# Two more pairs of heads in the later structure, in an attention and FFN kernel on one core

## The chip, the core and the metric

The kernel runs on one core of a Trainium2 chip. Five engines work side by side, each through its own instructions in order: TensorE (PE) multiplies matrices, VectorE (DVE) and ScalarE (ACT) work elementwise, GpSimd (POOL) does elementwise work more slowly, and SyncE (SP) issues the DMA transfers. The metric is the time of one execution on the device in microseconds (us). A difference under about 0.2% can't be told from no change here.

## What is computed

Attention with a block-causal mask over 8 batches of 8 heads, each 576 rows of 64, in float32; then a two-layer FFN over the 4608 rows of 512 that it yields.

```python
scores = scale * np.matmul(q, k.transpose(0, 1, 3, 2))
scores = np.where(block_i >= block_j, scores, -1000000000.0)      # blocks of 64
scores = scores - np.max(scores, axis=-1, keepdims=True)
attn = np.exp(scores)
attn = attn / (np.sum(attn, axis=-1, keepdims=True) + 1e-09)
x = np.matmul(attn, v)            # then heads side by side: (4608, 512)
h = x @ w_in                      # 512 -> 2048
out = np.maximum(0.01 * h, h) @ w_out
```

## The kernel before

**Heads.** The 64 heads are taken one after the other (`attention(i)`), rows in five tiles of up to 128 (`NT`). A head has scores in two groups (tiles 3 and 2, then 4, 1 and 0), each followed by a maximum over the row (DVE, L537), the exponential with its sum (ACT, L546), the reciprocal (DVE, L562 and L563) and, except in batch 0, the division of the rows (`normalising`, on POOL, DVE or ACT, L576 to L578). The rows are then turned, so that the keys lie on partitions, and a pair of heads is multiplied with v into `xr`, the FFN's input.

**Two structures.** Heads up to `PLAIN` (16 before: batches 0 and 1) use the early one: plain float32 scores from `k_in` and `qk_in` (L505), the rows turned by PE through `ident` (L603) and copied from PSUM to `ptf`, and the product with v in `paired` (L682). It has two sets of row buffers, `prow`. The heads from `PLAIN` on (`flip`) use the later one: q and k come in one load (L483), are split into a high and a low part (`qs`, `ks`), and the scores are products of those parts (L516); the rows are turned in 32 by 32 blocks on DVE into `turn` (L717), go out to `way` in DRAM (L732) and back into `ptm` (L739) so that the blocks land on their partitions, four DMAs each way a head; the product with v is in `columns` (L639). There is one set of `prow` for all of these heads.

**Weights.** `w_in` and `w_out` come as 64-bit words, in 32 pieces. `weight_piece` loads each into one of three `raw` buffers (L419) and decodes it in several steps through `val` (L272, L424, L428, L433 and, for every fifth, L437 and L438) into a high part (`wih`, `woh`) and the rest (`wil`, `wol`).

**FFN.** 18 chunks of 256 rows, each in eight steps u: `ffn1` multiplies x, split into `xh` and `xl`, with two columns of blocks of `w_in` (L795, 24 matmuls), then comes the activation (L810), the split of its result (`gh`, `gl`), and `ffn2` multiplies with `w_out` (L822, twice six matmuls) and adds up in `p_o` over the eight steps. A chunk can start when all heads of the batches that it reaches into are done: chunks 0 and 1 after batch 0, chunks 2 and 3 after batch 1, chunks 4 and 5 after batch 2. Chunks whose batch is done before head `PLAIN` use `xh0` alone; the later ones use `xh0` and `xh1` in turn.

**Memory that changes hands.** The early pool on the left holds the second `prow`, `ptf`, `vf`, `k_in` and `ident`; the coded pool on the right holds `raw` and `val`. At head `PLAIN`, `second_stage` closes the coded pool and puts the pool "late" there, once all weights are decoded; `third_stage` closes the early pool and puts the pool "last" there, once the early heads no longer use it.

**Order.** All steps are handed to `Plan`, which simulates the engines with written-out costs, and issues the instructions in the order that it finds. An operation has a rank; of those ready on an engine the lowest rank goes first. A head i has rank i and offsets of it (`RP`, `RB`, `RT`, `RV`, `RX`, `RN` for the division, `RM` for the DMAs to and from `way`); a weight piece has a rank between `OFF1` and `OFF1 + SL1`; an FFN step that of its head plus `LEAD`. `PADD`, `FILLTO` and `SPARE` are margins and limits within the plan. PE and the other engines each run what they were given in that order, so an instruction that waits holds up those behind it.

Of the kernel before, what the change touches and what calls it, by code (L numbers as in the profile page):

```python
# [9 lines left out]
F32 = mybir.dt.float32  # L10
F32R = mybir.dt.float32r
# [6 lines left out]
P = 128  # L18
BLK = 64
D = 64  # L20
S = 576
# [3 lines left out]
CH = 256  # L25
# [2 lines left out]
SIGNS = 5  # L28

WIDE = 512  # L30
PLAIN = 16
SPREAD = True

RAWS = 3
# [5 lines left out]
RT = 2.029  # L40
RV = 2.563
RX = -1.606
RN = -68.228
RM = -26.73

LEAD = 5.131
LAG = 1.993
RS = -9.988
RG = -0.7
OFF1 = 3.83  # L50
SL1 = 23.573
AHEAD = 2.641

MOVES = {
    "raw": (2200, 675), "first": (3300, 675), "v0": (1600, 900), "k": (900, 1170), "q": (500, 1110), "qk": (1500, 1325), "v": (450, 792),
    "way": (590, 385), "back": (1090, 1095), "out": (690, 354),
}
PADD = 2980.813
HOLD = 261.018
FILL = 235  # L60
FILLTO = -154.639


LOAD = 109
PAD = 510.012
PADO = 9.942
SPARE = 45.103
CHANGE = 100
RATE = 0.449
EDGE = 110  # L70
# [4 lines left out]
class Plan:  # L75
# [19 lines left out]
    def add(self, choices, rank, reads=(), writes=(), lag=None, kind=None):  # L95
        i = len(self.ops)
        deps = set()
        for k in reads:
            if k in self.writer:
                deps.add(self.writer[k])  # L100
        for k in writes:
            if k in self.writer:
                deps.add(self.writer[k])
            deps.update(self.readers.get(k, ()))
        for k in reads:
            self.readers.setdefault(k, []).append(i)
        for k in writes:
            self.writer[k] = i
            self.readers[k] = []
        deps.discard(i)  # L110
        self.ops.append((choices, rank, deps, lag, kind))

    def run(self):
# [16 lines left out]
        def offer(i):  # L130
            for k, choice in enumerate(self.ops[i][0]):
                e = choice[0]
                e = e[:3] if e == "DVE+" else e
                at = max([0] + [ends[d][1] + self.SYNC.get((ends[d][0], e), 0) for d in self.ops[i][2]])
                slack = {e: 0, "SP": PADD}
                spare = PAD if e == "PE" else PADO
# [32 lines left out]
        while done < total:  # L169
# [6 lines left out]
            for e, q in ready.items():  # L176
# [30 lines left out]
                if e == "DVE":  # L207
                    near, far = choices[k][3] if len(choices[k]) > 3 else (0, 0)
                    cost += EDGE * (near != edge)
                    edge = far  # L210
                free[e] = now + cost + SPARE
                if name in ("DVE+", "POOL"):
# [39 lines left out]
def attention_ffn(ctx: ExitStack, tc: tile.TileContext, q2: bass.AP, k2: bass.AP, qk: bass.AP, v: bass.AP, w_in: bass.AP, w_out: bass.AP, out: bass.AP):  # L252
# [3 lines left out]
    ND = DM // P  # L256
# [37 lines left out]
    def fixed(shape, dt, name, n=None, pool=const):  # L294
        if n is None:
            return pool.tile(shape, dt, name=name)
        return [pool.tile(shape, dt, name=f"{name}{i}") for i in range(n)]

    later = {}
# [11 lines left out]
    turned = 4 * BLK // 2 * slots  # L311
# [42 lines left out]
    xh = [fixed([P, ND, CH], F32R, "xh0")]  # L354
# [4 lines left out]
    pool = early.enter_context(tc.tile_pool(name="early", bufs=1, reuse_waits="tile"))  # L359
# [9 lines left out]
    pool = coded.enter_context(tc.tile_pool(name="coded", bufs=1, side="right", reuse_waits="tile"))  # L369
# [3 lines left out]
    def second_stage():  # L373
        coded.close()
        pool = ctx.enter_context(tc.tile_pool(name="late", bufs=1, side="right", reuse_waits="tile"))
        later["qs"] = fixed([P, S], F32R, "qs", 2, pool)
        later["ks"] = fixed([P, 2, S], F32R, "ks", None, pool)

    def third_stage():
        early.close()  # L380
        pool = ctx.enter_context(tc.tile_pool(name="last", bufs=1, reuse_waits="tile"))
        later["ptm"] = fixed([P, turned], F32, "ptm", 2, pool)
        later["turn"] = fixed([P, turned], F32, "turn", 2, pool)
        later["vt"] = fixed([P, NT, D], F32, "vt", 2, pool)
        xh.append(fixed([P, ND, CH], F32R, "xh1", None, pool))

    def weight_piece(num, rank, f, out_side, c0):
        w, k, kv = WIDE, num % RAWS, num % VALS
# [62 lines left out]
    def attention(i):  # L451
        b, h = divmod(i, H)
        z = i % 2
        r0 = float(i)
        flip = i >= PLAIN
        y = 0 if flip else z
# [9 lines left out]
        def pkeys(t):  # L466
            return [("p", y if t else 0, t)]
# [14 lines left out]
        else:  # L482
            add([("SP", ISSUE, lambda: nc.sync.dma_start(qk_in, qk[i - PLAIN]))], r0 - RL, [], ["qkt"], lag="qk")  # L483
            vt, vkey = lambda: later["vt"][z], ("vt", z)
# [37 lines left out]
        def softmax(tiles, mms, masks, r, both=None):  # L522
# [43 lines left out]
            for t, _, _ in () if scaled else tiles:  # L566
                add(normalising(t, qn[t]), r - RN, [("rec", z, at_col[t])], pkeys(t))

        def normalising(t, rr):
            by = rec[z][:rr, at_col[t] : at_col[t] + 1]  # L570

            def p():
                return row(t, rr, pc[t], kw[t])

            return [
                ("POOL", pool1(kw[t]), lambda: nc.gpsimd.tensor_scalar(p(), p(), by, 1.0, op0=ALU.mult, op1=ALU.mult)),  # L576
                ("DVE+", dve(kw[t], True) + 69, lambda: nc.vector.tensor_scalar_mul(p(), p(), by)),
                ("ACT", act(kw[t], True) + 108, lambda: nc.scalar.mul(p(), p(), by)),  # L578
            ]
# [125 lines left out]
    def turn(i, row, pkeys):  # L705
# [24 lines left out]
        for b in range(4):  # L730
            add(
                [("SP", ISSUE, lambda b=b: nc.sync.dma_start(way[z][b], later["turn"][z][:, b * w : (b + 1) * w]))],  # L732
                r0 + RM, ready, [("way", z, b)], lag="way",
            )
        for b in range(4):
# [4 lines left out]

            add([("SP", ISSUE, back)], r0 + RM, [("way", z, b)], [("ptm", z, b)], lag="back")

# [19 lines left out]
    def side(c):  # L762
        return 0 if ready[c] < PLAIN else (c + 1) % 2

    def split_x(c, rank):
        at = c * CH
        z = side(c)
        while at < (c + 1) * CH:
            b, o = divmod(at, S)
            ln = min(S - o, (c + 1) * CH - at)  # L770
            d = at - c * CH
            hi = [("xh", z, e) for e in range(d, d + ln, BLK)]
            keys = [("x", b % 2, h, y) for h in range(H) for y in (0, 1) if (o < 320 if y == 0 else o + ln > 320)]

            def part(which, b=b, o=o, ln=ln, d=d):
                return xr[b % 2][:, :, o : o + ln] if which is None else (xl if which else xh[z])[:, :, d : d + ln]

            x, top, low = (lambda part=part, y=y: part(y) for y in (None, 0, 1))
            add(copying(4 * ln, top, x, first="DVE"), rank, keys, hi)
            add(subtracting(4 * ln, low, x, top)[:1], rank, keys + hi, [("xl", e) for _, _, e in hi])  # L780
            at += ln
# [62 lines left out]
    for num, (f, o, c) in enumerate(pieces):  # L844
        kind = "wo" if o else "wi"
        wkeys.setdefault((kind, f), []).extend([((kind, f, c), 0), ((kind, f, c), 1)])
        weight_piece(num, OFF1 + SL1 * (num + 1) / len(pieces), f, o, c)
    ready = []
    for c in range(NCHUNK):
        b, o = divmod((c + 1) * CH - 1, S)  # L850
# [3 lines left out]
    for i in range(NH + 1):  # L854
        if i == H:
            add([("POOL", 1, narrow)], 0, [], [("h", y) for y in range(2)])
        if i == PLAIN:
            new = [("qs", y) for y in range(2)] + ["kh", "kl"]
            add([("POOL", 1, second_stage)], 0, [y for k in wkeys.values() for y in k], new)
            blocks = ((0, 0), (1, 0), (2, 0), (3, 0), (3, 3), (4, 0), (4, 3), (4, 4))  # L860
            new = [("turn", y, t, j) for y in range(2) for t, j in blocks]
            new += [("ptm", y, b) for y in range(2) for b in range(4)] + [("vt", y) for y in range(2)] + ["qkt"]
            new += [("xh", 1, e) for e in range(0, CH, BLK)]
            old = [("ptf", y, g[0]) for g in tgroups for y in range(2)] + ["ident"]
            old += [(k, y) for k in ("vf", "q", "k") for y in range(2)] + [("p", 1, t) for t in range(1, NT)]
            add([("POOL", 1, third_stage)], 0, [], sorted(set(old), key=str) + new)
        if i in events:
            here = [c for c in range(NCHUNK) if ready[c] == i]
            nxt = events[events.index(i) + 1] if i != events[-1] else i + H
            num = len(here) * NU  # L870
            for k in range(num):
                c, u = here[k // NU], k % NU
                rank = i + LEAD + (nxt - i) * k / num
                if u == 0:
                    split_x(c, rank - RS)
                ffn1(c, u, rank)
                ffn2(c, u, rank + (nxt - i) * LAG / num + 0.003)
        if i < NH:
            attention(i)
    if FILL:  # L880
# [3 lines left out]

        plan.fill = (FILL, fill, 2500, FILLTO)
    plan.run()
# [30 lines left out]
```

## Time and profile before

| | us |
|---|---|
| median of 3 runs (1067.55 to 1068.31) | 1067.56 |
| the profiled execution | 1069.45 |
| its span in the profile | 1067.7 |
| PE busy | 1051.8 |
| DVE busy | 552.7 |
| ACT busy | 549.8 |
| POOL busy | 316.3 |

The span runs from the first to the last instruction of the profiled execution; what lies around it is 1.75 us. The granted clock of PE is 1.00 of full speed, the upper of its two levels (2.4 GHz), in every slice of the page. Busy time is counted while an instruction is in flight; matmuls overlap, so an instruction's length in the trace is longer than what it adds to PE's time, and the distance between two starts is the better measure.

### The profile page before, as it was taken

What the parts mean: (1) busy time and instruction counts of PE and PEld (TensorE: products, weight loads), DVE (VectorE), ACT (ScalarE), POOL (GpSimd) and SP (SyncE); (2) the same over time, 40 slices, a digit from 0 to 9 for tenths busy, and PEclk for the clock granted to TensorE, in tenths of its full rate; (3) what the DMA queues carried; (4) which work ended last, traced back from release to release, by engine and by line L of the source; (5) the groups of instructions that cost most, each with busy time, mean ns of one, the idle gap of its engine ahead of it and who ended that gap; (6) DMA issues with size and microseconds to landing.
All of it is one profiled execution on the core that took longest, in us unless ns stands there. A gap on an engine that the chain in (4) does not pass through costs nothing.

```text
span 1067.7 us, 19239 instructions
## 1 busy us (share of the span) xinstructions
PE 1051.8 (99%) x7072; PEld 914.3 (86%) x7072; DVE 552.7 (52%) x1528; ACT 549.8 (51%) x1327; POOL 316.3 (30%) x304
## 2 busy tenths in 40 slices
PE   7899999999999999999999999999999999999998
PEld 5678888988888888888898888888898888999997
DVE  7998963566566676675444556556655520000000
ACT  7888864654555464554444555555555532222222
POOL 3454332432321222232121233323233322222221
PEclk9999999999999999999999999999999999999999
DMA  6555402776776687786266375667676650000000
GB/s 203 193 167 172 151 34 67 201 218 175 213 214 179 193 226 200 200 237 188 97 179 159 120 204 177 202 177 200 189 214 173 184 147 20 2 21 20 1 20 20
DMA packets 89885, 159.07 MB, mean 149 GB/s; under 512 B 9408, under 2 KB 74944, under 8 KB 89792
## 3 DMA queue, kind: packets, MB, share of 16 engines
q1 hardware_dynamic: 89792, 157.85, 50.7%
q8 instruction: 56, 0.92, 0.4%
q14 instruction: 37, 0.30, 0.1%
HBM read 104.33 MB, written 53.48 MB: 148 GB/s over the span
## 4 chain that ended last, share of the span: by engine, by line
PE 93%; DMA 2%; ACT 2%; DVE 2%; issue 0%; POOL 0%; SPq 0%; ACTq 0%; POOLq 0%
PE p_h L795 37%; PE p_o L822 36%; PE p_s L516 7%; PE p_t L639 6%; PE p_s L505 3%; PE p_t L603 1%; PE p_t L682 1%; DMA qk_in<-in_qk 1%; ACT prow L546 1%; DMA k_in<-in_k 1%; PE p_w L505 1%; DVE nmrec L537 1%; DMA way<-turn 0%; PE p_o L603 0%; DVE val L424 0%
## 5 line engine op out<-in xcount | busy, mean ns | idle before, releaser
L795 PE MATMUL p_h<-xh,wih 128*128 128x256 f32 x1152 | 317.4, 281 | 0.4 <-ACT xh L268 0.4
L795 PE MATMUL p_h<-xh,wil 128*128 128x256 f32 x1152 | 314.3, 278 | 0.0
L283 POOL TENSOR_TENSOR gl<-g,gh 128x512 fp32r<-128x512 f32 x130 | 169.4, 1303 | 468.0 <-ACT gh L268 370.4
L795 PE MATMUL p_h<-xl,wih 128*128 128x256 f32 x1152 | 300.0, 278 | 0.0
L795 PEld LDWEIGHTS p_h<-xh,wih 128*128 128x128 f32 x1152 | 216.5, 188 | 12.5 <-issue 3.2
L795 PEld LDWEIGHTS p_h<-xh,wil 128*128 128x128 f32 x1152 | 217.0, 188 | 0.5
L795 PEld LDWEIGHTS p_h<-xl,wih 128*128 128x128 f32 x1152 | 208.0, 188 | 8.2 <-issue 0.3
L810 ACT ACTIVATE g<-p_h 128x512 f32<-128x512 f32 x144 | 85.9, 597 | 242.3 <-PE p_h L795 242.0
L546 ACT ACTIVATE prow<-p_s,nmrec 128x448 f32<-128x448 f32 x300 | 154.2, 523 | 69.1 <-DVE nmrec L537 68.0
L822 PE MATMUL p_o<-woh,gh 128*128 128x512 f32 x576 | 181.4, 396 | 0.0
L822 PE MATMUL p_o<-wol,gh 128*128 128x512 f32 x576 | 179.3, 392 | 0.0
L822 PE MATMUL p_o<-woh,gl 128*128 128x512 f32 x576 | 179.2, 392 | 0.0
L717 DVE STREAM_TRANSPOSE turn<-prow 128x128 f32<-128x128 f32 (+3 forms) x384 | 143.0, 402 | 49.5 <-POOL prow L576 42.4
L822 PEld LDWEIGHTS p_o<-woh,gl 128*128 128x128 f32 x576 | 108.2, 188 | 24.3
L822 PEld LDWEIGHTS p_o<-wol,gh 128*128 128x128 f32 x576 | 108.2, 188 | 23.5
L537 DVE TENSOR_REDUCE nmrec<-p_s 128x1 f32<-128x448 f32 x300 | 127.5, 469 | 1.2
L576 POOL TENSOR_SCALAR prow<-prow,nmrec 128x448 f32<-128x448 f32 (+3 forms) x98 | 70.4, 720 | 186.1 <-DVE nmrec L563 127.9
L822 PEld LDWEIGHTS p_o<-woh,gh 128*128 128x128 f32 x576 | 89.7, 188 | 4.9 <-issue 2.7
L516 PE MATMUL p_s<-ks,qs 128*128 128x288 f32 (+4 forms) x528 | 91.6, 306 | 0.9 <-ACT prow L546 0.9
L282 DVE TENSOR_TENSOR xl<-xr,xh 128x1024 fp32r<-128x1024 f32 (+3 forms) x24 | 22.6, 950 | 128.2 <-PE p_h L795 128.1
L516 PEld LDWEIGHTS p_s<-ks,qs 128*128 128x128 f32 x528 | 78.9, 188 | 8.8 <-issue 1.9
L268 ACT CAST gh<-g 128x512 fp32r<-128x512 f32 x123 | 76.2, 619 | 19.9 <-PE p_o L822 18.0
(96 smaller groups left out, 995.9 us busy)
## 6 DMA issues: line engine op xcount, KB each, us to landing
way<-turn SPq DMA_DIRECT2D x192, 224.0 KB, 2.5
ptm<-way SPq DMA_DIRECT2D x192, 224.0 KB, 4.6
qk_in<-in_qk SPq DMA_DIRECT2D x48, 576.0 KB, 4.5
out<-ob SPq DMA_DIRECT2D x35, 256.0 KB, 2.6
raw<-in_w_in SPq DMA_DIRECT2D x16, 512.0 KB, 4.3
raw<-in_w_out SPq DMA_DIRECT2D x16, 512.0 KB, 3.8
vt<-in_v SPq DMA_DIRECT2D x48, 160.0 KB, 4.8
vf<-in_v SPq DMA_DIRECT2D x16, 160.0 KB, 2.7
```

Source lines behind the costliest of these rows:

```text
L268: one = lambda: nc.scalar.copy(dst(), src())
L283: ("POOL", pool2(n), lambda: nc.gpsimd.tensor_sub(dst(), one(), two())),
L505: go = lambda ap=ap, cols=cols, k0=k0, k1=k1, first=first, last=last: nc.tensor.matmul(ap, q_of()[:, cols], kt()[:, k0:k1], start=first, s ...
L516: nc.tensor.matmul(ap, later["qs"][z][:, cols], moving, start=first, stop=last)
L537: [("DVE", dve(kw[t]), lambda t=t, ap=ap, flat=flat: nc.vector.tensor_reduce(nm[z][: qn[t], at_col[t] : at_col[t] + 1], ap[: qn[t]], axis= ...
L546: nc.scalar.activation(o, ap[: qn[t]], AF.Exp, bias=nm[z][: qn[t], at_col[t] : at_col[t] + 1], scale=1.0, accum_out=sums[z][: qn[t], at_co ...
L576: ("POOL", pool1(kw[t]), lambda: nc.gpsimd.tensor_scalar(p(), p(), by, 1.0, op0=ALU.mult, op1=ALU.mult)),
L639: nc.tensor.matmul(dst, later["vt"][z][:, j], src, start=start, stop=stop)
L717: nc.vector.transpose(dst, src.rearrange("p (s b i) -> p s b i", b=4, i=32))
L795: nc.tensor.matmul(p_h[z][:, i, :], w[:, d, f * P : (f + 1) * P], (xl if x else xh[y])[:, d, :], start=first and k == 0 and (u > 0 or i == ...
L810: add([("ACT", act(512), lambda: nc.scalar.activation(g, p_h[z], AF.Prelu, alpha=0.01))], rank, [("h", z)], ["g"])
L822: nc.tensor.matmul(p_o[m], a[:, i, m * P : (m + 1) * P], w[:, 2 * u + i, :], start=u == 0 and k == 0, stop=u == NU - 1 and k == 5,)
```

## The change

`PLAIN` goes from 16 to 12. Heads 12 to 15, the second half of batch 1, take the later structure. `qs` and `ks` move from the pool "late" into the pool "last", and `turn` and `xh1` move from "last" into "late". So `turn` and `xh1` now lie where the weights were decoded, `qs` and `ks` where the early heads had their buffers, and the lists of what each stage hands over change with them. The constants of the plan are set anew, which changes the order of the instructions on every engine.

```diff
-PLAIN = 16
+PLAIN = 12
...
-RN = -68.228
-RM = -26.73
+RN = -79.904
+RM = -25.225
...
-SL1 = 23.573
+SL1 = 24.252
...
-PADD = 2980.813
+PADD = 2346.17
...
-FILLTO = -154.639
+FILLTO = -146.062
...
-SPARE = 45.103
+SPARE = 46.259
...
     def second_stage():
         coded.close()
         pool = ctx.enter_context(tc.tile_pool(name="late", bufs=1, side="right", reuse_waits="tile"))
-        later["qs"] = fixed([P, S], F32R, "qs", 2, pool)
-        later["ks"] = fixed([P, 2, S], F32R, "ks", None, pool)
+        later["turn"] = fixed([P, turned], F32, "turn", 2, pool)
+        xh.append(fixed([P, ND, CH], F32R, "xh1", None, pool))

     def third_stage():
         early.close()
         pool = ctx.enter_context(tc.tile_pool(name="last", bufs=1, reuse_waits="tile"))
         later["ptm"] = fixed([P, turned], F32, "ptm", 2, pool)
-        later["turn"] = fixed([P, turned], F32, "turn", 2, pool)
+        later["qs"] = fixed([P, S], F32R, "qs", 2, pool)
+        later["ks"] = fixed([P, 2, S], F32R, "ks", None, pool)
         later["vt"] = fixed([P, NT, D], F32, "vt", 2, pool)
-        xh.append(fixed([P, ND, CH], F32R, "xh1", None, pool))
...
         if i == PLAIN:
-            new = [("qs", y) for y in range(2)] + ["kh", "kl"]
+            blocks = ((0, 0), (1, 0), (2, 0), (3, 0), (3, 3), (4, 0), (4, 3), (4, 4))
+            new = [("turn", y, t, j) for y in range(2) for t, j in blocks] + [("xh", 1, e) for e in range(0, CH, BLK)]
             add([("POOL", 1, second_stage)], 0, [y for k in wkeys.values() for y in k], new)
...
+            new = [("qs", y) for y in range(2)] + ["kh", "kl", "qkt"] + [("vt", y) for y in range(2)]
+            new += [("ptm", y, b) for y in range(2) for b in range(4)]
```

## Rows read from the trace of the kernel before

**Rows 1.** The page: busy time by engine, a costly group, and a DMA's landing.

```profile
PE 1051.8 (99%) x7072; PEld 914.3 (86%) x7072; DVE 552.7 (52%) x1528; ACT 549.8 (51%) x1327; POOL 316.3 (30%) x304
...
L717 DVE STREAM_TRANSPOSE turn<-prow 128x128 f32<-128x128 f32 (+3 forms) x384 | 143.0, 402 | 49.5 <-POOL prow L576 42.4
...
ptm<-way SPq DMA_DIRECT2D x192, 224.0 KB, 4.6
```

**Rows 2.** Waits of PE, the longest: us in total, times, longest us.

```profile
PE p_s L505 <- ACT k_in L271: 4.4, 1, 4.4
```

**Rows 3.** Windows: stretch and length, then busy us of PE, PEld, DVE, ACT, POOL, clock, DMA.

```profile
100.00:150.00 50.00, 50.00 (x317) 40.89 (x316) 43.55 (x99) 37.94 (x94) 17.12 (x14) 1.00 0.39 121
150.00:200.00 50.00, 50.00 (x335) 44.28 (x334) 20.23 (x59) 25.60 (x64) 16.91 (x16) 1.00 0.27 85
```

**Rows 4.** Timeline of PE: start and length in us, line, operation, tiles.

```profile
101.72 1.62 PE L505 MATMUL p_s<-k_in,qk_in 128*128 128x288 f32 x8
103.15 0.71 PE L822 MATMUL p_o<-woh,gh 128*128 128x512 f32 x2
103.71 0.62 PE L822 MATMUL p_o<-wol,gh 128*128 128x512 f32 x2
...
108.77 1.45 PE L505 MATMUL p_s<-k_in,qk_in 128*128 128x448 f32 x4
109.81 0.87 PE L822 MATMUL p_o<-woh,gh 128*128 128x512 f32 x2
110.53 0.63 PE L822 MATMUL p_o<-wol,gh 128*128 128x512 f32 x2
...
111.45 1.04 PE L603 MATMUL p_t<-ident,prow 128*128 128x128 f32 x8
112.24 0.37 PE L795 MATMUL p_h<-xh,wih 128*128 128x256 f32 x1
...
126.71 0.93 PE L603 MATMUL p_t<-ident,prow 128*128 128x128 f32 x7
127.39 0.71 PE L822 MATMUL p_o<-woh,gh 128*128 128x512 f32 x2
...
177.50 0.87 PE L516 MATMUL p_s<-ks,qs 128*128 128x448 f32 x4
...
182.42 1.03 PE L516 MATMUL p_s<-ks,qs 128*128 128x288 f32 x7
183.28 0.62 PE L822 MATMUL p_o<-woh,gh 128*128 128x512 f32 x2
...
188.82 0.86 PE L516 MATMUL p_s<-ks,qs 128*128 128x448 f32 x4
189.52 0.62 PE L822 MATMUL p_o<-woh,gh 128*128 128x512 f32 x2
```

**Rows 5.** The chain that ended last, in order of time: start and length in us.

```profile
118.88 2.84 PE p_t L682 x20
...
164.80 1.40 PE p_o L822 x6
166.20 2.84 PE p_t L682 x20
...
203.69 1.84 PE p_h L795 x16
...
217.71 2.96 PE p_t L639 x28
```

**Rows 6.** Windows of 103 to 143: DVE, ACT, POOL on `val` alone; then all engines.

```profile
103.00:143.00 40.00, 24.65 (x38) 9.07 (x14) 7.78 (x6) 1.00 0.43 132
...
103.00:143.00 40.00, 40.00 (x248) 33.30 (x246) 36.61 (x81) 30.86 (x73) 13.98 (x11) 1.00 0.43 132
```

**Rows 7.** Timelines of POOL (the last weight) and of SP (the first pair's `ptm`).

```profile
141.39 1.65 POOL L283 TENSOR_TENSOR wol<-val,woh 128x512 fp32r<-128x512 f32 x1 [3.67 <-DVE woh L269]
...
206.00 2.40 SPq L739 DMA_DIRECT2D ptm<-way  x4
```

More of the change, by code (lines that the diff above doesn't have):

```diff
@@ L857, in attention_ffn @@
         if i == PLAIN:
-            new = [("qs", y) for y in range(2)] + ["kh", "kl"]
+            blocks = ((0, 0), (1, 0), (2, 0), (3, 0), (3, 3), (4, 0), (4, 3), (4, 4))
+            new = [("turn", y, t, j) for y in range(2) for t, j in blocks] + [("xh", 1, e) for e in range(0, CH, BLK)]
             add([("POOL", 1, second_stage)], 0, [y for k in wkeys.values() for y in k], new)
[L860 to L863, printed above, removed]
+            new = [("qs", y) for y in range(2)] + ["kh", "kl", "qkt"] + [("vt", y) for y in range(2)]
+            new += [("ptm", y, b) for y in range(2) for b in range(4)]
             old = [("ptf", y, g[0]) for g in tgroups for y in range(2)] + ["ident"]
```

## The prediction

> **What bounds the kernel now.** I read the page's first part, then TensorE's (PE's) waits, then the windows, then PE's own timeline. PE is busy 1051.8 of 1067.7 us [rows 1], so 15.9 us of the span is not PE work; the longest wait, 4.4 us, is the first one, on k at the start [rows 2]. From 100 to 200 us PE has no idle time at all, while VectorE (DVE) falls from 43.6 busy us in 100 to 150 to 20.2 in 150 to 200 [rows 3]. So work taken off PE shortens the span, unless PE then waits for something. The whole question is whether it does, and the place to look is 100 to 200 us, where the early structure ends and the later one begins.
>
> A check that PE's time is understood. Sixteen matmuls of the first FFN product take 1.84 us, so a piece of 12 takes 1.38, and a piece of six of the second takes 1.40 [rows 5]; an eighth of a chunk has two of each, 5.56 us, a chunk 44.5, all 18 some 801. That leaves some 250 us for the 64 heads, and only they are touched.
>
> **PE work removed: 11.4 us.** The price of an instruction group is the distance from its start to the start of what follows, since matmuls overlap; a change of structure also slows the group behind it, and that is counted too.
> - An early head has two groups of scores. The eight-matmul one runs 101.72 to 103.15, 1.43 us, and the pair behind it takes 0.56 instead of 0.47 (a third of 1.40), so 1.52. The four-matmul one runs 108.77 to 109.81, 1.04, and the pair behind takes 0.72, so 1.29. [rows 4, 5]
> - It has 15 transposes on PE: 0.79 us for eight and 0.68 for seven [rows 4]. The change behind them I take at the same 0.09 each (the two measured values are 0.09 and 0.25): 1.65. Sum for an early head: 4.46.
> - A later head has 0.70 for four and 0.86 for seven score matmuls, 1.56, and no PE transposes [rows 4].
> - So 2.90 us a head, 11.6 for four. The product with v goes the other way: a pair takes 2.96 instead of 2.84 us [rows 5], 0.24 more for two pairs. Net **11.4 us**. With change-overs of 0.25 behind the transposes it would be 12.7, with none at all 9.7; I keep 11.4.
>
> **Work added elsewhere.** Each of the four heads gets eight DVE transposes at 402 ns, 3.2 us [rows 1], eight more DMA issues on SP (four for `way`, four for `ptm`; four of the latter take 2.40 us [rows 7]), a joint load of q and k, and the split of q and k; it loses the copies of PE's transposes out of PSUM. From 150 us on DVE works 20.2 us of 50 [rows 3], so four times 3.2 us fits there and I cost it at nothing. If it had to run before the weights are decoded, DVE would have no room (43.6 of 50) and it would cost its full length in decoding time; that is the term below. On SP the new loads stand in one queue with the loads of raw weights: a load of q and k that waits for its buffer holds the raw loads queued behind it, and with them the decode.
>
> The transposes take 1.65 us a head on the engine that is 99% busy and 3.2 us on one that is 52% busy [rows 1], so the rows speak for the move. A rule speaks against it: the Trainium skill, VectorE: DVE Perf Modes, section Rules for kernel authors, gives a 128x128 transpose to TensorE where PSUM will do as the target, since VectorE turns 32x32 blocks only. By that rule the four heads would keep their 6.6 us on PE, and the gain would be 4.8 us instead of 11.4.
>
> **What takes the place: the decode of the weights.** `second_stage` puts the transposed rows' buffers (`turn`) where raw and decoded weights lie, so no new head can be turned before the last weight is decoded; today that is at 143.0 (141.39 + 1.65) [rows 7]. Chunk 0 of the FFN needs all the weights as well, and chunk 1 can't begin its second product before chunk 0 is through (one pair of accumulators, and one `xh` for both). So taking heads 12 to 15 out of 103 to 143 us only helps if the decode gets faster.
> - In 103 to 143 DVE works 36.61 us, a share of 0.915; 24.65 of it on weights [rows 6], 11.96 on the rest, most of it heads 12 to 14. The new head 12 can start only near 130 (below). I take a third of the 11.96 to stay: 28.6 us at the same share is 31.3 us, decode ends at **T = 134.3**. None left gives 129.9, all left 143.0: the bounds.
> - From T on PE has: the last eighth of chunk 0's, less its first half, 4.2 us; chunk 1, 44.5; scores of heads 13 to 15, 4.7; two products with v, 5.9; the scores of heads 16, 17 and half of 18, which today also stand ahead of chunk 2, 3.8; less 2.8 of chunk 1 that runs behind the start of chunk 2. Sum 60.3, so chunk 2 starts at 134.3 + 60.3 = 194.6.
> - Today chunk 2 starts at 203.7 [rows 5]; with 11.4 us of work gone and no new idle time it would be 192.3. So **2.3 us of new idle time**. With T at 132.0 or less there is none; with T at 143 it would be 11.0.
>
> **Is the attention there in time?** Chunk 2 is the first to need heads 12 to 15. Today the last early product with v starts at 166.2 and the first scores of the new structure at 177.50, 11.3 us later; the product of that first new pair comes at 217.7, 40.2 later; a head follows the one before by 11.3 us (177.50 to 188.82) [rows 4, 5]. The last early product moves to heads 10 and 11, at 118.9 [rows 5]. So first new scores at 130.2, first pair 170.4, second pair 22.6 later: 193.0. That is what it takes with PE coming late: the last `ptm` transfer of the first new pair is issued by 208.4 [rows 7] and with the median 4.6 us to land [rows 1] it is in at 213.0, 4.7 before PE takes it. So 188.3 to 193.0, and with 3 us for the product chunk 2 can start from 191.3 to 196.0. The decode's 194.6 lies within that, so the two clocks agree, and I keep 2.3. The copy and cast of x hide behind the last 2.8 us of chunk 1.
>
> **Sum.** The profiled execution took 1069.45 us (span 1067.7 and 1.75 around it); less 11.4, plus 2.3: 1060.35. The three runs have a median of 1067.56, 1.89 below the profiled one, so on their scale the forecast is 1067.56 - 9.1 = **1058.5 us**.
>
> **Rivals.**
> - Full gain: the decode ends by 132.0 and the attention keeps its 188.3. For it: DVE and ACT are relieved of three heads just there. Then 1067.56 - 11.4 = 1056.2, and 1055 with the dearer change-overs or a shorter start (15.9 us of idle time, which a new order can shift by a little either way).
> - The attention is late: the steps between heads stretch from 11.3 to 13 us because the new heads start beside the decode. Four steps cost 6.8 us more, so chunk 2 starts between 198.1 and 202.8 instead of 191.3 and 196.0; the middle, 200.5, is 8.2 us of idle time: 1064.3.
> - Slower than before, from one mechanism: the turn of head 12 waits for the decode, and there is one set of `prow` buffers for all new heads, so head 13 can't write its rows until head 12 is turned. Today the product of the first pair comes 35.3 us after the second scores of its first head (182.42), which is about when its turning can start. If the decode still ends at 143.0, the products come at 178.3 and, 22.6 later, 200.9, and chunk 2 at 203.9: the whole gain is gone, 1067.8. From there each us of T costs a us: if head 12's own softmax, which the planner ranks ahead of weights, pushes the decode to 147, the time is 1071.5. For it: DVE is nearly full there today. Against: the new head cannot start until near 130, so it pushes less than the three heads that it replaces.
> - A later hand-over from one batch to the next turns tight because PE comes to it earlier. No row here prices that; it widens the upper end.
>
> **How the numbers follow.** Forecast with 1 to 4.5 us of new idle time, 1057.5 to 1061: 0.54. Full gain, 1055 to 1057.5: 0.16. Attention late, 1061 to 1065.4: 0.13. Gain gone, 1065.4 to 1069.7 (within 0.2%, about what can be told from no change here): 0.09. Slower: 0.08. The range that leaves out no more than 2 in 10 is 1055.5 to 1066. Faster 0.83, same 0.09, slower 0.08.
>
> **What would show it.** Right: PE busy near 1040 us (11 to 12 less), 60 fewer transposes of L603 and 32 more of L717; last write of `wol` between 130 and 138; chunk 2's first group of 16 near 195; some 2 to 4 us of new PE waits between 120 and 200, on weights (`wih`, `woh`) or on `ptm` or `xh`. Wrong: PE's busy time not down by 11 (prices wrong), the last decode at 143 or later, or a wait of PE of over 8 us ahead of chunk 2.

## The result and the profile after

The changed kernel takes **1074.08 us** (median of five runs, 1073.07 to 1076.25) against 1067.77 of the kernel before, measured beside it: 1.0056 times as long, interval 1.0042 to 1.007. It is slower, by 6.3 us. The forecast of 1058.5 was 15.6 us too low, and the range of 1055.5 to 1066 doesn't hold the time. The profiled execution took 1076.25 us, the longest of the five, with a span of 1074.2 (before 1067.7).

The page of the kernel after, the lines that answer to [rows 1]:

```profile
span 1074.2 us, 19255 instructions
...
PE 1052.8 (98%) x7024; PEld 914.0 (85%) x7024; DVE 562.1 (52%) x1558; ACT 550.2 (51%) x1327; POOL 317.1 (30%) x308
...
L717 DVE STREAM_TRANSPOSE turn<-prow 128x128 f32<-128x128 f32 (+3 forms) x416 | 155.7, 403 | 64.5 <-POOL prow L576 53.6
```

PE has 48 instructions fewer and DVE 32 more transposes, as foreseen, and yet PE is busy 1.0 us longer than before instead of 11 less. Its idle time (span less busy) rose too, from 15.9 to 21.4 us.

Windows of after, the stretches of [rows 3] and [rows 6]:

```profile
100.00:150.00 50.00, 49.79 (x329) 43.45 (x328) 44.52 (x88) 33.93 (x75) 16.34 (x13) 1.00 0.45 146
103.00:143.00 40.00, 39.79 (x261) 34.28 (x260) 35.92 (x65) 26.95 (x58) 12.16 (x9) 1.00 0.44 144
150.00:200.00 50.00, 49.15 (x326) 42.83 (x326) 32.01 (x99) 27.97 (x71) 17.59 (x16) 1.00 0.74 206
```

This is where the prediction looked, and hardly anything is lost there: PE idles 1.06 us in 100 to 200. DVE takes the new work in 150 to 200 (32.0 us instead of 20.2) without holding PE up. The loss is elsewhere.

**Where the time went, by line.** Below is a reading of our own of the two traces: for each line of PE the distances from one matmul's start to the next, less the idle time between them, added up (rounded); "ends" is what lies before the first and behind the last matmul. The columns are the kernel before, and the differences from it for after and for two experiments that come below.

```
us                          before   after    e7      e9
L505 early scores             47.8    -9.0   -10.6    -9.8
L603 transposes on PE         26.1    -4.8    -6.0    -5.5
L516 later scores             76.5    +6.9    +6.7    +6.8
L639, L682 products with v    93.6    +0.2    +0.2    +0.2
L795 first FFN product       402.4    +6.4    +1.8    +0.2
L822 second FFN product      400.8    +1.3    -0.5    -0.7
idle between matmuls           7.7    +5.4    +3.5    +6.5
ends, L671                    12.8     0       0      -0.1
span                        1067.7    +6.5    -4.9    -2.6
```

The heads gave back 6.7 us (the first four lines), but the FFN, in which no instruction was changed, takes 7.7 us more, and 5.4 us of idle time are new. A stretch at a lower clock, shown below, adds some 3.4 us to after alone, in L505, L603 and L795; so a part of the 7.7 and of what the heads lack is the clock's. So there are two questions: why the FFN is slower, and where PE idles.

**The FFN's step.** Timeline of PE, single sixteenths of a chunk (12 matmuls of L795, six of L822); start and length in us. First before, in chunk 16:

```profile
978.20 0.28 PE L795 MATMUL p_h<-xh,wih 128*128 128x256 f32 x1
...
979.59 0.62 PE L822 MATMUL p_o<-woh,gh 128*128 128x512 f32 x2
...
980.96 0.28 PE L795 MATMUL p_h<-xh,wih 128*128 128x256 f32 x1
```

After, first in chunk 13, which reads `xh0`, then in chunk 14, which reads `xh1`:

```profile
851.05 0.28 PE L795 MATMUL p_h<-xh,wih 128*128 128x256 f32 x1
...
852.44 0.62 PE L822 MATMUL p_o<-woh,gh 128*128 128x512 f32 x2
...
853.81 0.28 PE L795 MATMUL p_h<-xh,wih 128*128 128x256 f32 x1
...
903.42 0.28 PE L795 MATMUL p_h<-xh,wih 128*128 128x256 f32 x1
...
904.84 0.62 PE L822 MATMUL p_o<-woh,gh 128*128 128x512 f32 x2
...
906.23 0.28 PE L795 MATMUL p_h<-xh,wih 128*128 128x256 f32 x1
```

Twelve matmuls of L795 take 1.39 us before and in chunk 13 of after, but 1.42 in chunk 14; the whole sixteenth 2.76, 2.76 and 2.81. Sixteen times 0.05 is 0.8 us a chunk, and eight chunks (2, 4, ... 16) read `xh1`. The mean step from one L795 matmul to the next is 114.6 to 116.0 ns before, in every chunk; after, it is 118.5 to 118.9 in the even chunks from 2 on and 115.4 to 116.3 in the odd ones up to 13. The clock is 1.00 and PE counts as busy throughout, so no busy share shows it; the number of matmuls does. Windows of 900 to 950 (before in the first fence, after in the second):

```profile
900.00:950.00 50.00, 50.00 (x333) 45.71 (x332) 1.63 (x3) 12.46 (x20) 12.82 (x10) 1.00 0.03 11
```

```profile
900.00:950.00 50.00, 50.00 (x324) 45.45 (x323) 1.63 (x3) 12.46 (x20) 11.61 (x9) 1.00 0.03 12
```

**The new idle time** is not at the hand-over at 130 to 200 but at 70 to 85, where chunk 0 starts. Windows, before in the first fence and after in the second:

```profile
70.00:80.00 10.00, 9.45 (x73) 8.42 (x72) 9.86 (x22) 9.64 (x22) 5.53 (x5) 1.00 0.63 187
80.00:90.00 10.00, 10.00 (x66) 8.64 (x65) 8.44 (x20) 9.12 (x23) 4.54 (x5) 1.00 0.52 157
```

```profile
70.00:80.00 10.00, 6.39 (x41) 4.83 (x39) 9.56 (x22) 8.47 (x21) 4.25 (x4) 1.00 0.57 166
80.00:90.00 10.00, 8.54 (x40) 6.79 (x41) 8.53 (x17) 5.66 (x17) 2.53 (x3) 0.66 0.45 149
```

PE loses 3.1 us in the first of these windows and 1.5 in the second, and then the granted clock falls: in this execution 6.8 us from 81.0 on run at the lower level (1.2 GHz; 0.66 in 80 to 90), which costs half of that, some 3.4 us. The chain of after in that stretch, and in two fences of their own the split of x on DVE, in after and then in before:

```profile
74.63 3.38 DMA raw<-in_w_out
...
78.09 0.69 ACT val L271
...
79.15 0.68 DVE val L428
79.83 0.60 DVE wol L282
80.44 0.60 DVE val L433
...
81.90 2.23 DVE xl L282
...
84.17 2.08 PE p_h L795 x8
```

```profile
81.81 2.30 DVE L282 TENSOR_TENSOR xl<-xr,xh 128x1024 fp32r<-128x1024 f32 x1
```

```profile
73.97 1.22 DVE L282 TENSOR_TENSOR xl<-xr,xh 128x1024 fp32r<-128x1024 f32 x1
```

With the new constants DVE decodes more pieces of a weight before it splits chunk 0's x: `xl` starts at 81.8 instead of 74.0. The longest of PE's waits there is not the one for `xl` itself. Timeline of PE, after and then, in a fence of its own, before:

```profile
80.76 2.72 PE L505 MATMUL p_s<-k_in,qk_in 128*128 128x448 f32 x4 [2.22 <-ACT prow L546]
...
84.17 2.08 PE L795 MATMUL p_h<-xl,wih 128*128 128x256 f32 x8 [0.70 <-DVE xl L282]
```

```profile
76.50 1.17 PE L795 MATMUL p_h<-xl,wih 128*128 128x256 f32 x8
```

Before, PE has the products with `xl` from 76.50 on while ACT is at the exponentials. In after they aren't ready, and the next scores in its order wait 2.22 us for the exponential that frees their buffer. This is 50 us before the first of the four heads that changed.

### The profile page after: what moved, and what is told of

Same layout as the page of the kernel before. It is cut to its first block, busy times and chain, and to the rows that moved or that the text cites. A ratio compares the mean times of both kernels' runs of the same rounds, so it can differ in the third digit from the quotient of the medians.

```text
span 1074.2 us, 19255 instructions
## 1 busy us (share of the span) xinstructions
PE 1052.8 (98%) x7024; PEld 914.0 (85%) x7024; DVE 562.1 (52%) x1558; ACT 550.2 (51%) x1327; POOL 317.1 (30%) x308
## 4 chain that ended last, share of the span: by engine, by line
PE 86%; DVE 5%; DMA 5%; ACT 2%; issue 1%; POOL 0%; SPq 0%; ACTq 0%; POOLq 0%; DVEq 0%
PE p_h L795 34%; PE p_o L822 34%; PE p_s L516 7%; PE p_t L639 6%; DMA qk_in<-in_qk 3%; PE p_s L505 1%; ACT prow L546 1%; DVE nmrec L537 1%; PE p_t L603 1%; PE p_t L682 1%; DMA raw<-in_w_out 1%; PE p_w L505 1%; DMA out<-ob 1%; DVE val L428 1%; DVE turn L717 1%
## 5 line engine op out<-in xcount | busy, mean ns | idle before, releaser
L795 PE MATMUL p_h<-xh,wih 128*128 128x256 f32 x1152 | 318.8, 282 | 0.2 <-DVE xh L269 0.2
L795 PE MATMUL p_h<-xh,wil 128*128 128x256 f32 x1152 | 316.5, 280 | 0.0
L795 PE MATMUL p_h<-xl,wih 128*128 128x256 f32 x1152 | 303.1, 281 | 0.7 <-DVE xl L282 0.7
L283 POOL TENSOR_TENSOR gl<-g,gh 128x512 fp32r<-128x512 f32 x127 | 165.5, 1303 | 451.9 <-ACT gh L268 367.9
L795 PEld LDWEIGHTS p_h<-xh,wih 128*128 128x128 f32 x1152 | 216.8, 188 | 12.8 <-issue 2.9
L795 PEld LDWEIGHTS p_h<-xh,wil 128*128 128x128 f32 x1152 | 217.9, 189 | 0.6
L795 PEld LDWEIGHTS p_h<-xl,wih 128*128 128x128 f32 x1152 | 208.9, 189 | 9.8 <-DVE xl L282 1.6
L717 DVE STREAM_TRANSPOSE turn<-prow 128x128 f32<-128x128 f32 (+3 forms) x416 | 155.7, 403 | 64.5 <-POOL prow L576 53.6
L822 PE MATMUL p_o<-woh,gh 128*128 128x512 f32 x576 | 181.1, 396 | 0.2 <-ACT ob L268 0.2
L822 PE MATMUL p_o<-wol,gh 128*128 128x512 f32 x576 | 180.1, 394 | 0.0
L822 PE MATMUL p_o<-woh,gl 128*128 128x512 f32 x576 | 179.2, 392 | 0.0
L822 PEld LDWEIGHTS p_o<-woh,gl 128*128 128x128 f32 x576 | 108.2, 188 | 25.1
L822 PEld LDWEIGHTS p_o<-wol,gh 128*128 128x128 f32 x576 | 108.2, 188 | 24.3
L537 DVE TENSOR_REDUCE nmrec<-p_s 128x1 f32<-128x448 f32 x300 | 127.4, 469 | 1.2
L516 PE MATMUL p_s<-ks,qs 128*128 128x288 f32 (+4 forms) x572 | 99.9, 308 | 1.5 <-ACT prow L546 1.5
L822 PEld LDWEIGHTS p_o<-woh,gh 128*128 128x128 f32 x576 | 90.6, 188 | 4.6 <-issue 1.9
L516 PEld LDWEIGHTS p_s<-ks,qs 128*128 128x128 f32 x572 | 83.7, 189 | 10.7 <-ACT prow L546 3.7
L268 ACT CAST gh<-g 128x512 fp32r<-128x512 f32 x128 | 79.2, 619 | 19.8 <-PE p_o L822 17.7
```

Source lines behind the costliest of these rows:

```text
L268: one = lambda: nc.scalar.copy(dst(), src())
L283: ("POOL", pool2(n), lambda: nc.gpsimd.tensor_sub(dst(), one(), two())),
L516: nc.tensor.matmul(ap, later["qs"][z][:, cols], moving, start=first, stop=last)
L537: [("DVE", dve(kw[t]), lambda t=t, ap=ap, flat=flat: nc.vector.tensor_reduce(nm[z][: qn[t], at_col[t] : at_col[t] + 1], ap[: qn[t]], axis= ...
L717: nc.vector.transpose(dst, src.rearrange("p (s b i) -> p s b i", b=4, i=32))
L795: nc.tensor.matmul(p_h[z][:, i, :], w[:, d, f * P : (f + 1) * P], (xl if x else xh[y])[:, d, :], start=first and k == 0 and (u > 0 or i == ...
```

## The experiments

Two theories of the slower FFN: **the address** of `xh1`, which changed its pool (bytes per partition: 214080 before, 225248 after; `xh0` 172608 and `xl` 176704 in both), or **the order** that the new constants give. Since matmuls are compared within a kernel, single runs are read by their step, not by their time; runs of one kernel lie up to 5.2 us apart (e9: 1066.2 to 1071.43). A spacer is a tile that nothing reads or writes; it moves addresses, and the order of instructions stays.

**e1**, after with `xh1` 32 bytes lower, at a multiple of 64:

```diff
-        xh.append(fixed([P, ND, CH], F32R, "xh1", None, pool))
+        xh.append(fixed([P, ND, CH], F32R, "xh1", None, pool)); fixed([P, 8], F32, "spacer", None, pool)
```

> The changed kernel with a spacer of 32 bytes at the end of the pool on the right, so that xh1 (and turn) start 32 bytes lower, on a multiple of 64 bytes as xh1 did before the change; all five engines' instructions and their order are the same. Theory A (xh1's start): in the changed kernel the 12-matmul pieces of L795 step by 118.8 ns in the chunks that read xh1 (2, 4, ... 16) and by 115.6 in those that read xh0. With xh1 on 64 both step by 115.6; eight chunks of 192 matmuls at 3.2 ns are 4.9 us, so 1069.2 against 1074.1 of the changed kernel. Rival (the step drifts from run to run, or depends on which side of the memory the tile lies): it stays at 1074.1 and the alternation by chunks stays or changes without order.

1071.88 us, 1.0035 (1.0021 to 1.0049). The step in the even chunks fell to 117.4 ns, not to 115.5: the address matters, but a multiple of 64 is not what it takes.

**e2**, before with the same spacer ahead of `xh1` (214112):

```diff
-        xh.append(fixed([P, ND, CH], F32R, "xh1", None, pool))
+        fixed([P, 8], F32, "spacer", None, pool); xh.append(fixed([P, ND, CH], F32R, "xh1", None, pool))
```

> The kernel before with a spacer of 32 bytes ahead of xh1, which then starts 32 bytes past a multiple of 64; nothing else moves, the order is the same. Theory A: chunks 2, 4, ... 16 step by 118.8 ns instead of 115.6, 4.9 us more, 1072.6. Rival (drift, or the side of the memory): 1067.7.

1075.03 us, 1.0062 (1.0048 to 1.0076). An empty tile of 32 bytes makes the kernel before as slow as the change does. The even chunks' step is 118.5 ns, the odd ones' unchanged; by line, as in the table above, L795 takes 5.0 us more and L822 1.3. The address theory holds, and the loss is more than expected; the place of `xh1` alone is worth as much as the whole difference between the two kernels.

**e3**, after with the six constants of before, and **e4**, the same with e1's spacer:

```diff
-RN = -79.904
-RM = -25.225
+RN = -68.228
+RM = -26.73
...
-SL1 = 24.252
+SL1 = 23.573
...
-PADD = 2346.17
+PADD = 2980.813
...
-FILLTO = -146.062
+FILLTO = -154.639
...
-SPARE = 46.259
+SPARE = 45.103
```

> The changed kernel with the constants of the plan as before the change (RN, RM, SL1, PADD, FILLTO, SPARE); xh1 stays off 64. PE's order is then that of the kernel before up to the scores of head 12. Theory B (the refitted order at the start): in the changed kernel the split of chunk 0's x comes later (xl at 81.8 instead of 74.0 us), PE idles 5.5 us more up to 205 us and runs 6.8 us at half clock, some 3.4 us lost. With the old order that is back: 8 to 9 us less, 1065 to 1066. Rival C (the forecast's own place: decode of the weights and late attention at the hand-over, 120 to 200 us): the loss stays there whatever the start looks like, 1072 to 1076.

> Both: old constants and xh1 on 64. Theories A and B together: 1074.1 - 4.9 - 8.5 = 1060.7, and PE's own work 11.4 us below that of the kernel before, less what new waits take from it. Rival C: no better than 1068.

e3 1072.06 us, 1.0031 (1.0019 to 1.0042); e4 1068.4, 1.0001 (0.9992 to 1.0009). Both missed, high by 6 to 8 us. The early waits at 70 to 85 are gone in both, so these do come from the constants. But PE waits elsewhere instead, which the expectations left out: at the hand-over, the place of rival C. Windows, after in the first fence and e3 in the second:

```profile
130.00:143.00 13.00, 12.79 (x79) 11.14 (x78) 11.29 (x18) 8.23 (x18) 7.01 (x5) 1.00 0.23 75
```

```profile
130.00:143.00 13.00, 9.17 (x49) 7.78 (x48) 11.47 (x26) 8.70 (x22) 7.98 (x7) 0.87 0.23 77
```

In e3 PE idles 3.8 us here and the clock falls, in after it idles 0.2; e4 has 9.15 us at a clock of 0.87. So the constants move a wait from one place to the other, and the net of it is 2.0 us between after and e3. In e4 the even chunks' step, 117.4 ns where 115.6 was expected, is missing from the gain as well.

**e5** and **e6**, before with `xh1` 64 and 128 bytes further, both multiples of 64:

```diff
-        xh.append(fixed([P, ND, CH], F32R, "xh1", None, pool))
+        fixed([P, 16], F32, "spacer", None, pool); xh.append(fixed([P, ND, CH], F32R, "xh1", None, pool))
```

(e6 has 32 in place of 16.)

> The kernel before with xh1 64 bytes higher, at 214144: on a multiple of 64 and of 128; before it was at 214080, 64 past a multiple of 256. Read from the profile alone: the step of L795 in chunks 2, 4, ... 16 (115.5 ns before, 118.5 at 32 bytes off, 117.4 at 225216 in the changed kernel). If only the start within 64 bytes matters, 115.5. If the start within 128 or 256 does, another step. If it is which part of the memory xh1 lies in, 115.5, and 225216 is bad for its place.

> The kernel before with xh1 128 bytes higher, at 214208, 192 past a multiple of 256, as 225216 is in the changed kernel with the 32 byte spacer. If the start within 256 bytes matters: 117.4 ns in chunks 2, 4, ... 16. If only 64 bytes or the part of the memory: 115.5.

1075.4 and 1076.59 us, one execution each, beside 1068.88; the even chunks' step is 118.2 and 117.4 ns. So not only multiples of 64 but the place within 256 bytes counts. By now 64 above a multiple of 256 (before) is good, and 96, 128, 192 and 224 are not.

**e7**, e4 with a spacer of 160 bytes, so that `xh1` lies at 225088, again 64 above a multiple of 256:

```diff
-        xh.append(fixed([P, ND, CH], F32R, "xh1", None, pool))
+        xh.append(fixed([P, ND, CH], F32R, "xh1", None, pool)); fixed([P, 40], F32, "spacer", None, pool)
```

> The changed kernel with the old constants and a spacer of 160 bytes, so that xh1 starts at 225088, 64 past a multiple of 256 as in the kernel before; order unchanged against the run with 32 bytes. If the start within 256 bytes matters: 115.5 ns in chunks 2, 4, ... 16 instead of 117.4, 2.9 us less in L795 and about 1 less in L822, 1064.5 against 1068.4. If it is the part of the memory: 117.4 and 1068.4 as with the spacer of 32 bytes.

**1065.21 us, 0.9961 (0.9947 to 0.9976)**: faster than both kernels, as expected. The step is 115.3 to 116.3 ns in all chunks from 2 on. The four heads' new structure, without the two things that came with it, is a gain of 0.4%. Its page, PE's waits (us in total, times, longest), and the chain at the hand-over:

```profile
PE 1043.5 (98%) x7024; PEld 908.8 (86%) x7024; DVE 565.7 (53%) x1563; ACT 549.6 (52%) x1323; POOL 318.0 (30%) x307
```

```profile
PE p_s L505 <- ACT k_in L271: 4.5, 1, 4.5
PE p_s L516 <- ACT prow L546: 4.3, 3, 2.1
```

```profile
133.31 1.30 POOL wil L283
...
134.65 1.43 PE p_h L795 x10
...
136.10 0.60 ACT g L810
136.70 1.41 ACT prow L546 x6
...
138.16 0.96 PE p_s L516 x4
...
139.13 3.68 PE p_h L795 x16
```

PE waits here for the decode after all, by a detour: POOL finishes a piece of `wil`, PE multiplies with it, ACT activates the result, and only behind that come the exponentials that free the buffer for the scores of head 13. After the last of these waits 16 matmuls take 3.68 us instead of 1.84 [rows 5]; the granted clock in 139 to 143 is 0.57, so most of it ran at the lower level (1.2 GHz):

```profile
139.00:143.00 4.00, 3.99 (x19) 3.83 (x19) 3.92 (x12) 2.27 (x5) 0.71 (x2) 0.57 0.28 110
```

**e8** moves `xh0`, `xl` and `xh1` of before by 64 bytes together (all 128 above a multiple of 256, as the weights are); **e11** by 192 (all at a multiple of 256); **e12** puts the spacer of 64 ahead of `wih`, so that weights and x (and every tile behind them in that pool) move together and the weights come to 192:

```diff
-    xh = [fixed([P, ND, CH], F32R, "xh0")]
+    fixed([P, 16], F32, "spacer"); xh = [fixed([P, ND, CH], F32R, "xh0")]
```

```diff
-    wih = fixed([P, ND, DFF], F32R, "wih")
+    fixed([P, 16], F32, "spacer"); wih = fixed([P, ND, DFF], F32R, "wih")
```

(e11 has e8's line with 48.)

> The kernel before with 64 bytes of spacer ahead of xh0, so that xh0, xl and xh1 all start 128 past a multiple of 256 instead of 64; order as before. Read from the profile: L795's step. If what counts is that xh1 has the same start within 256 bytes as xl, with which it alternates: 115.5 ns in all chunks, as before. If the start itself counts (64 past a multiple of 256 is good, the others not): 117 to 118.5 in all chunks, odd ones too, some 10 us more.

> The kernel before with 192 bytes of spacer ahead of xh0: xh0, xl and xh1 all start on a multiple of 256 (before: 64 past it; with 64 more, 128 past it, the step was 119.3 ns in all chunks). The weights stay at 128. If each start within 256 bytes has its own step: some step between 114 and 119.5 in all chunks; a step under 115.5 would be a layout better than both kernels'.

> The kernel before with 64 bytes of spacer ahead of wih, so that the weights (128 to 192 past a multiple of 256) and xh0, xl and xh1 (64 to 128) move together. If what counts is where x starts relative to the weights: 115.5 ns in all chunks, about 1068. If the start of x itself counts: 119.3 in all chunks, as with x alone moved by 64, about 1082.

e8 1082.81 us, e11 1083.44, e12 1071.12; the kernel before took 1068.71 beside the first and 1068.32 beside the others. Each of the three is a single execution, so they are read by their step. Timelines of PE, a sixteenth of e8 in chunk 16, then one of e12:

```profile
989.62 0.28 PE L795 MATMUL p_h<-xh,wih 128*128 128x256 f32 x1
...
991.06 0.63 PE L822 MATMUL p_o<-woh,gh 128*128 128x512 f32 x2
...
992.45 0.28 PE L795 MATMUL p_h<-xh,wih 128*128 128x256 f32 x1
```

```profile
979.88 0.28 PE L795 MATMUL p_h<-xh,wih 128*128 128x256 f32 x1
...
981.27 0.62 PE L822 MATMUL p_o<-woh,gh 128*128 128x512 f32 x2
...
982.64 0.28 PE L795 MATMUL p_h<-xh,wih 128*128 128x256 f32 x1
```

In e8 the twelve matmuls take 1.44 us, in e12 1.39 as before. Its x lies at 128, as in e8; what differs is where the weights lie. So the address of x alone doesn't decide; what fits is the distance between the two operands. All runs together (own reading: place of a tile's start within 256 bytes, and the mean L795 step of the chunks that read it):

```
run              x read     x   weights   x - weights   step, ns
before           xh0, xh1   64    128        192         115.5
e7, e9, e10      xh1        64    128        192         115.4 to 116.3
e12              xh0, xh1  128    192        192         115.9
e2               xh1        96    128        224         118.5
e5               xh1       128    128          0         118.2
e8               xh0, xh1  128    128          0         119.3
e1, e4, e6       xh1       192    128         64         117.4
after, e3        xh1       224    128         96         118.6
e11              xh0, xh1    0    128        128         119.1
```

In e8, e11 and e12 `xl` moved along; in the others it stayed at 64. Of six distances tried, one is good. But e12 is the only run with the weights at another place, and its other tiles moved too: that weights at 192 suit x at any place would fit as well, and no run tells the two apart. e12's 1071.12 is one run, whose L795 is 1.6 us above before; e12 is not shown to be quite as good as before.

**e9** and **e10** take the other half, the constants, at the good address: e9 is after with e7's spacer, e10 the same with `SPARE` alone as before:

```diff
-SPARE = 46.259
+SPARE = 45.103
```

> The changed kernel, its own constants, with xh1 at 225088 (64 past a multiple of 256); order as in the changed kernel. L795 at 115.5 ns throughout; 1074.1 less 7 (3.1 ns on 1536 matmuls of L795, 1.6 ns on 768 of L822 and what goes with it): 1067 to 1068. The gap to the run with old constants and the same address (1065.2) is then what the refit costs: 2 to 3.5 us, as between the two pairs of runs so far (1074.1 and 1072.1; 1071.9 and 1068.4).

> As the run before this one, but SPARE 45.103 as before the change; the other five constants stay refitted. PE's order at the start is then that of the kernel before up to the scores of head 12, so the idle time between the start of chunk 0 and 90 us is gone. If the refit's loss is this shift of chunk 0's split: 1065 to 1066, as with all old constants. If it is elsewhere: 1067 to 1068.

e9 1068.24 us, 0.9995 (0.9984 to 1.0006); e10 1066.1, 0.997 (0.9958 to 0.9982): 0.2 and 0.1 us above the ranges expected. Windows, e9 in the first fence and e10 in the second:

```profile
70.00:80.00 10.00, 6.31 (x41) 4.91 (x40) 9.59 (x22) 8.65 (x22) 3.93 (x4) 1.00 0.57 184
80.00:90.00 10.00, 8.14 (x57) 7.05 (x58) 9.55 (x19) 7.46 (x17) 2.53 (x3) 1.00 0.39 124
```

```profile
70.00:80.00 10.00, 9.26 (x74) 8.54 (x73) 9.86 (x21) 9.98 (x24) 5.24 (x5) 1.00 0.53 162
130.00:143.00 13.00, 10.15 (x65) 8.31 (x64) 11.70 (x26) 8.63 (x21) 7.61 (x7) 1.00 0.22 74
```

`SPARE`, a margin of the plan, alone makes the early gap: with its old value PE is busy 9.26 us of 70 to 80, against 6.31, and idles 2.85 us at the hand-over instead. From after to e9 is 5.8 us for the address; from e9 to e10 2.1 for `SPARE`; from e10 to e7 0.9 for the other five, which is within what these runs can tell. The 2.1 us rest on the medians of 12 executions each: e10's profiled execution, 1068.38 us, is the longest of its 12, and by our own reading idles 14.3 us in all against e9's 14.2, so the traces show that the wait moves and not what that gains.

## Why the prediction was wrong

The forecast gained 9.1 us; the changed kernel lost 6.3. Of the 15.6 us between forecast and result 5.8 are the address (after to e9) and 3.0 the constants (e9 to e7). Of the 6.7 that are left between e7 and the forecast, 4.2 are found by line below and 1.3 come from the kernel before, which took 1068.88 beside e7 and not 1067.56; the last 1.2 is how far the two profiled executions lie from their medians (before 0.6 above, e7 0.6 below). The kernels were timed on different occasions; taken as ratios to the kernel before beside each, the address is 6.5 us, the constants 3.6, and e7 lacks 4.9 of the gain forecast. Point by point:

- **The bound, right.** PE stayed the bound and DVE, ACT and POOL took the added work at no cost that shows at 150 to 200. The check that PE's time is understood was done for the kernel before only; the same check on the kernel after, a chunk's sixteenth of 2.81 instead of 2.76 us, is what would have told the rest.
- **The step that failed: what the change of the pools costs.** The prediction said "some 250 us for the 64 heads, and only they are touched", and took the exchange of the two pools as a matter of when memory becomes free. It had no term for where a tile lies. In after the 800 us of FFN became 7.7 us longer, where the address alone gives 6.3 (e2, L795 and L822); moving `xh1` by 160 bytes gives 5.8 us back (after to e9), and moving it by 32 bytes in the kernel before costs 0.62% (e2). No row of the trace of before could give this price, since both of its x tiles lie at the good distance. It could have been bounded only as an unknown of a moved operand, and wasn't.
- **The refit constants, not priced.** They stand in the change as "set anew", and the prediction let a new order shift the idle time "a little either way". It was 2 to 3 us of the loss (after to e3 2.0, e9 to e7 3.0), most of it `SPARE`'s by the medians. Late `xl` makes the early wait; what the old constants have in its place is the wait at the hand-over.
- **Work off PE, 11.4 us: right in kind, too large.** By e7's account the heads' lines fall by 9.7 (early scores 10.6, forecast 11.2; transposes 6.0, forecast 6.6; later scores 6.7 more, forecast 6.2; products as forecast), and L822 by 0.5, where part of the change-overs was counted. So 10.2. The forecast charged a dearer change-over than the change of structure really gives back. Two of its sums are off, though neither enters the forecast: with no change-over at all its own terms give 9.3 us, not 9.7, and a decode that ends at 147 gives 1071.8, not 1071.5. The Trainium skill, VectorE: DVE Perf Modes, section Rules for kernel authors, would have kept the transposes on TensorE; e7 has 60 fewer of them there, 6.0 us less of L603, and behind the decode, where DVE does its 32 more, PE idles 0.98 us of 143 to 200. Here the measurement decides against that rule, for a kernel bound by PE.
- **The decode and the hand-over, 2.3 us of idle time: right in place, too small.** The last `wol` was to be written by 134.3. In e7 it ends at 138.2, in after at 142.3:

```profile
140.81 1.48 POOL L283 TENSOR_TENSOR wol<-val,woh 128x512 fp32r<-128x512 f32 x1 [3.94 <-ACT woh L268]
```

  The estimate let the decode move up into the room that three heads left, with 4.0 us of DVE's other work to stay. Windows of e7 up to the end of its decode, all engines and then `val` alone (DVE, ACT, POOL):

```profile
103.00:138.18 35.18, 31.34 (x202) 26.26 (x200) 31.64 (x59) 25.13 (x55) 11.95 (x9) 1.00 0.51 160
...
103.00:138.18 35.18, 21.71 (x33) 10.70 (x18) 8.89 (x7) 1.00 0.51 160
```

  DVE is as full as forecast (a share of 0.90), but 9.9 us of it are other work: mostly the maxima of scores (L537, 3.3), `gh` and `gl` of the FFN (3.9) and the split of q and k of the new heads (2.8; their lengths overlap a little). That is the term that was mis-sized. New idle time is 3.5 us in e7 (forecast 2.3), with some 1.8 us more from the lower clock behind it, which the forecast hadn't at all. Together with the smaller work this makes up e7's shortfall: its span is 4.9 us below before, the forecast said 9.1; 1.2 is work, 1.2 idle time, 1.8 L795.
- **The attention's clock, right.** First new scores were forecast at 130.2, the first new product at 170.4; e7 has 129.29 and 170.34. The second product comes at 196.0 (forecast 193.0 at the latest). In after they come at 135.4, 178.0 and 198.7, since it starts late.
- **Chunk 2 near 195, wrong.** It starts at 205.4 in after and 202.7 in e7, only about 1 us earlier than before [rows 5], and yet e7 gains. What stands ahead of it in PE's order changed, so the start of one chunk was no measure of the gain.
- **The rivals.** None was the cause. The slower one (the turn of head 12 waiting for the decode) ends with a late chunk 2, by 11 us of idle time. After shows two of its signs, a decode that ends at 142.3 and a chunk 2 at 205.4, but not the idle time: PE idles 1.06 us in 100 to 200. Slower had 0.08, for the wrong mechanism.

**Open.** Why the place of the operands matters is not known; only that it does. In after and e3 the odd chunks at the very end (15 and 17) have a step of 117.7 ns although they read `xh0`; in e1, where `xh1` lies 32 bytes lower, they have 115.4. L822 is slower there too, 232 ns instead of 229 in before's last chunks, and its operands didn't move; and in after's even chunks the step from a matmul that reads `xh1` to one that reads `xl` is longer as well, 117.9 ns instead of 116.0. So the operands of one matmul by themselves don't explain its step. The clock is open too: e9 has the early gap and stays at 1.00 in its trace, though by the mean clock of each execution six of its 12 were at 0.997 or 0.998, and three of the five of after, all six of e7 and eight of the 12 of e10 at 0.998 or less, against two of 23 of the kernel before beside them. Where it fell in those without a trace isn't on record.

## What to carry to other kernels

When a change moves an operand of the main matmuls to another pool, compare its address and that of the other operand before and after, and measure the step from start to start in an untouched loop: busy shares don't show it. Keep the constants of a fitted order fixed when a structure is tried, and fit them behind it, so that the two can be told apart; and when a wait goes away, look where the next one comes up. A gain on the bound engine is worth what is left when all its lines, the unchanged ones too, have been added up.

## What the runs showed of the hardware

- The step of back-to-back matmuls of 128x128 by 256 columns (the type shown as fp32r) depends on where their operands start. In these runs the place of x relative to the weights within 256 bytes orders it: on average 115.4 to 116.3 ns at a distance of 192, and 117.4 to 119.3 at the other five tried, at the same granted clock of 1.00; the exceptions are chunks 15 and 17 of after and e3 (117.7 at 192). Thirty-two bytes cost this kernel 0.6% (e2), 64 bytes for all x tiles 1.3% (e8, one execution: 1082.81 against 1068.71). The Trainium skill, SBUF — State Buffer, section Operand start alignment, asks of a start only that it be a multiple of the element's size, and says that its runs timed nothing; every start here satisfies it, so the rule is about what is allowed, and speed is another matter.
- PE's granted clock fell to the lower level behind some waits and not behind others like them: in after behind one of 2.22 us that ended at 80.8 (clock 0.66 in 80 to 90), in e7 behind one of 2.09 us that ended at 138.2 (0.57 in 139 to 143); in e9, with 1.75 and 1.86 us at 78 to 83, it stayed at 1.00. Where it fell, the loss behind the gap, some 3.4 and 1.7 us, was of the size of the gap.
